# Third batch: crossbar transposes on SyncE's queue in place of TensorE transposes

## The chip, the cores and the metric

One core of one Trainium2 chip runs the whole program. The metric is device time in microseconds, the median of a few runs. A profiled execution has a span of its own, from the first to the last instruction, and a time of its own, which is a little longer. Engines are named as the profile names them: PE (TensorE matmuls), PEld (weight loads), DVE (VectorE), ACT (ScalarE), POOL (GpSimd), SP (SyncE). A name with a q (SPq, ACTq) is the engine's sequencer, which issues DMAs.

## The reference

A retention layer without softmax, then a two-layer network with a swish of learned slope. There are 8 batches, 8 heads, 576 positions and 64 columns for each head. Flattened, that is 4608 tokens of 512 columns.

```python
scores = scale * np.matmul(q, k.transpose(0, 1, 3, 2))
gamma = 1.0 - 2.0 ** (-5.0 - np.arange(H, dtype=np.float32))
Dmat = np.where(rel >= 0, gamma[:, None, None] ** rel[None, :, :], 0.0)
attn = np.matmul(scores * Dmat, v)
x = attn.transpose(0, 2, 1, 3).reshape(B * S, H * D)
h = x @ w_in                            # 512 -> 2048
out = (h * sigmoid(beta * h)) @ w_out   # 2048 -> 512
```

## The kernel before

The decay `gamma ** (s - t)` is split into a factor for the query and one for the value, so that only the causal mask is left between them. Each batch has 512 main positions, in four chunks of 128, and a tail of 64; two tails make a chunk of their own. The list `seq` numbers all chunks: batch b, chunk c is number 4b + c up to number 15, then come two tail chunks, and so on. The third batch, batch 2, has the chunks 8 to 11, taken as two pairs, (8, 9) and (10, 11). Chunks within a batch are joined by a state of 64x64 for each head, which `a_st` sums up and ScalarE copies into one of three buffers `sbds`.

For one batch the work is this. `load_q` (L81) fetches the queries in two DMAs of 512 KB, `load_kv` (L94) fetches keys and values of one chunk in two DMAs of 256 KB, all on SyncE's queue. POOL scales the queries (`pre_q`, L247), casts the keys (`pre`, L273) and scales the values (L255). Then queries and keys are turned, so that the head's columns lie on partitions. There are two ways to do that:

- On TensorE: `t_q` (L297) makes 8 transposes and one copy from PSUM (L298), twice in a batch, once with the copy on ScalarE and once with it on VectorE. `t_k` (L303) makes 4 transposes for one chunk and one copy on ScalarE (L304).
- By a DMA through the crossbar: `x_q` turns half the queries of a batch, `x_k` a pair of key chunks, `x_tail` a chunk of tails. All call `turn` (L281), which issues one transpose of 256 KB from ScalarE's queue.

The constant `XB = 3` says from which batch on the second way is taken. Then `first` does `a_st` and the scores `a_sc` of a pair (L323, masked by VectorE at L333), and `outputs` does for all four chunks `a_O` (L366), `a_cross` (L351, needs the states in `sbds`) and `a_x` (L384), the copy of the result to `xT`, on ScalarE for chunk 1 of a batch and on VectorE for the others.

The network's two layers are the bulk: `up` (L413) with its swish on ScalarE (L415), `down` (L426) with its copy on VectorE (L433) and its store on SyncE's queue (L436). Together they are the list `fill`. The order of all instructions on all engines is fixed by hand: `merged` walks through `fill`, and ahead of the entry of index n it emits every step of the other streams whose place is at most n. Each engine, and each DMA queue, takes its instructions in that order, and an instruction that waits holds back those behind it on the same engine. The indices that matter here: `d0` = 16 is the first `down` of batch 0, whose last entries for its four blocks of rows are at 25, 26, 27 and 31; `u1` = 32 is the first `up` of batch 1, in halves of 256 columns up to index 51; 58 to 73 are the `down` of batch 1, with stores after 61, 65, 69 and 73; `base[2]` = 74 is the first `up` of batch 2.

In the kernel before, the third batch has these places. POOL emits `pre_q(2)` at 41 to 44 and `pre` of chunks 8 to 11 at 46.5 to 48. `t_q` is at 47.5 and 48.5, `t_k` at 49.5, 50.5, 58.5 and 59.5, `first(8)` at 53, `a_st(9)` at 55, `first(10)` at 62, `outputs(8)` at 67. For the fourth batch, `load_q(3)` is at 47, `load_kv(12)` and `load_kv(13)` at 49 and 51, `pre_q(3)` at 57 to 60, `pre(12)` and `pre(13)` at 61 and 62, `x_q(3, 0)` at 63, `x_q(3, 1)` at 64.5, `x_k(3, 0)` at 66.5, `first(12)` at 77.

Of the kernel before, what the change touches and what calls it, by code (L numbers as in the profile page):

```python
# [19 lines left out]
def kernel(  # L20
# [10 lines left out]
    nc = tc.nc  # L31
# [9 lines left out]
    CB = MB // P  # L41
# [25 lines left out]

    NQ = 6
    E = CB
    XB = 3  # L70
    QB = 2
    q_tiles, kv_tiles = {}, {}

# [158 lines left out]
    batch, pair, live = {}, {}, {}  # L232
# [44 lines left out]
    def heads(t, p):  # L277
        return t[:, 2 * p:2 * p + 2, :].rearrange("p h d -> p (h d)")

    def turn(dst, src):  # L280
        nc.scalar.dma_start_transpose(dst.rearrange("p j pr s -> p (j pr) s"), src.rearrange("p j h d -> p (j h d)"))  # L281

    def x_q(b, u):
        turn(batch[b]["qT"][:, 2 * u:2 * u + 2], batch[b]["qs"][:, 2 * u:2 * u + 2])

    def x_k(b, u):
        kn, kT = pair[b, u]
        turn(kT, kn)

    def x_tail(i):  # L290
        turn(live[i]["qkT"], live[i]["qk"])
# [122 lines left out]
                             start=(ko == 0), stop=(ko == KO - 1))  # L414
        nc.scalar.activation(gts[m][:, fo, :, w], ph, ACT.Silu, scale=beta_sb[:, fo:fo + 1])  # L415

    pos_, ots = {}, {}

    def down(m, ms, f0, fn=4, n0=0, nn=d_model):

        gT = gts[m]
        if f0 == 0:
            pos_[ms] = psum.tile([P, d_model], F32, name="po", tag="mm", bufs=3)
        po = pos_[ms]
        for fo in range(f0, f0 + fn):
            nc.tensor.matmul(po[:, :nn], gT[:, fo, ms, :], w_out_sb[:, fo, n0:n0 + nn],  # L426
                             start=(fo == 0), stop=(fo == FO - 1))
        if f0 + fn < FO:
            return
        if ms == 0:  # L430
            ots[m] = stage.tile([P, MB // P, d_model], F32, name="ot", tag="wt", bufs=4)
        ot = ots[m][:, ms, n0:n0 + nn]
        nc.vector.tensor_copy(ot, po[:, :nn])  # L433
        if m < B:
            rows = out[m * S:m * S + MB].rearrange("(s i) n -> s i n", i=CB)
            nc.sync.dma_start(rows[:, ms, n0:n0 + nn], ot)  # L436
        else:
            for x in range(2):
                r0 = (2 * ms + x) * S + MB
                nc.sync.dma_start(out[r0:r0 + TL, n0:n0 + nn], ot[x * TL:(x + 1) * TL])  # L440
# [12 lines left out]
    def F(f, *a):  # L453
        return lambda: f(*a)
# [49 lines left out]
    fill = [F(up, 0, fo) for fo in range(FO)]  # L504
    d0 = len(fill)
    fill += [F(down, 0, ms, f0) for f0 in range(0, FO, 4) for ms in range(3)]
    fill += [F(down, 0, 3, f0) for f0 in range(0, FO, 4)]

    u1 = len(fill)
    fill += [F(up, 1, fo, 2 * x, 2) for x in range(2) for fo in range(10)]  # L510
    fill += [F(up, 1, fo) for fo in range(10, FO)]
    fill += [F(down, 1, ms, f0) for ms in range(MB // P) for f0 in range(0, FO, 4)]
    base = {1: u1 + 10}
    for n, m in enumerate(blocks[2:], 2):
# [6 lines left out]
    def second(i):  # L521
        for f in (a_O, lambda j: a_cross(j, False), a_x):
# [6 lines left out]
               [(d0 - 4 + 3.3 * g, F(cast_w_out, g)) for g in range(WG)],  # L529
               [(10.3, F(load_q, 1))] + [(10.3, F(load_kv, CB + n, (j,))) for n, j in keys_first],  # L530
               [(10.4, F(load_q, 2))] + [(10.4, F(load_kv, 2 * CB + n)) for n in range(2)],
               [(d0 + 8.6, F(load_kv, 2 * CB + 2)), (d0 + 10.1, F(load_kv, 2 * CB + 3))],
               [(d0 + 7, F(pre_q, 1, n)) for n in range(4)] + [(d0 + 10.6, F(t_q, 1, 0)), (d0 + 12.6, F(t_q, 1, 1))],
               [(d0 + 8, F(pre, 4, (0,))), (d0 + 8, F(pre, 5, (0,))), (d0 + 9, F(pre, 4, (1,))), (d0 + 9, F(pre, 5, (1,))),
                (d0 + 12.7, F(t_k, 4)), (d0 + 12.8, F(t_k, 5)), (d0 + 13.8, F(a_sc, 4)), (d0 + 13.81, F(a_sc, 5)),
                (d0 + 14.8, F(a_st, 4)), (d0 + 15.9, F(second, 4))],
# [16 lines left out]
    def pair_prep(i, at):  # L553
        b, c = seq[i]
        if b is None:
            return [(at - 31, F(load_tail, c)), (at - 21.5, F(pre, i)), (at - 21, F(load_tail, c + 1)),
                    (at - 13, F(pre, i + 1)), (at - 12, F(x_tail, i)), (at - 9.5, F(x_tail, i + 1))]
        n, st = full.index(i), []
        if b < XB:
            if c == 0:  # L560
                st += [(at - 12 + x, F(pre_q, b, x)) for x in range(4)]
                st += [(at - 5.5, F(t_q, b, 0)), (at - 4.5, F(t_q, b, 1))]
                st += [(at - 6.5 + x / 2, F(pre, i + x)) for x in range(CB)]
            return st + [(at - 3.5, F(t_k, i)), (at - 2.5, F(t_k, i + 1))]
        if c == 0:
            st += [(at - 30, F(load_q, b))] + [(at - 20 + x, F(pre_q, b, x)) for x in range(4)]
            st += [(at - 14 + 1.5 * x, F(x_q, b, x)) for x in range(2)]
        return st + [(at - 28, F(load_kv, n)), (at - 26, F(load_kv, n + 1)), (at - 16, F(pre, i)),
                     (at - 15, F(pre, i + 1)), (at - 10.5, F(x_k, b, c // 2))]

    todo = list(range(2 * CB, len(seq), 2))
    for n in range(1, B - 1):

        take = [i for i in todo if seq[i][0] == n + 1 or n == B - 2 or seq[i] == (None, 0) and n == CB - 1]
        todo = todo[len(take):]
        lo, hi = (base[n] + 11, base[n + 1] - 12) if n == 1 else (base[n] + 3, base[n + 1] - 8)
        at = [lo + x * (hi - lo) / (len(take) - 1) for x in range(len(take))]
        if len(take) == 2 and n > 1:
            at[1] -= 6
        for i, t in zip(take, at):  # L580
            st = pair_prep(i, t) + [(t, F(first, i))]
            if seq[i][0] is None:
                st.append((t + 5, F(second, i)))
            elif seq[i][1] == 0:
                st.append((t + 2, F(a_st, i + 1)))
            else:
                st.append((t + 5, F(outputs, i - 2)))
            streams.append(st)
# [32 lines left out]
```

## Time and profile before

| What | Value |
|---|---|
| median of 3 runs | 311.66 us (311.6 to 312.2) |
| the profiled execution: its time | 311.92 us |
| the profiled execution: its span | 310.1 us |
| granted TensorE clock, mean | 0.998 |
| ACT busy | 143.0 us (46%) |
| DVE busy | 106.9 us (34%) |
| POOL busy | 96.0 us (31%) |
| transposes of queries on PE, L297 | 48, of them 16 in batch 2 |
| transposes of keys on PE, L303 | 48, of them 16 in batch 2 |
| crossbar transposes on ACT's queue, L281 | 24 |

PE's own rows count a matmul from its start to its modelled end, and matmuls overlap; so the time that a group takes from PE is read from the chain of waits, where pieces follow one another without overlap. In a row of the timeline the columns are start, duration, engine, line, operation, output<-input, and the number of instructions merged; in brackets is the idle time ahead of it and what ended that. For a DMA the duration is that of its issue on the sequencer; the time to landing is told apart.

### The profile page before, as it was taken

The numbers are of one execution on the slowest core, as the hardware profiler recorded it, in microseconds if no ns is written. First come the engines' busy times: TensorE is split into PE (matmuls) and PEld (weight loads), VectorE is DVE, ScalarE is ACT, GpSimd is POOL, SyncE is SP. The second block draws the span as 40 slices with busy tenths as digits, with TensorE's granted clock in tenths as the row PEclk, the third lists the DMA queues.
The fourth block names the chain that finished last, engine by engine and source line by source line (L and its number), as shares of the span: only waits on it lengthen the run. The fifth ranks groups of instructions, "written<-read, shape, count | busy, mean of one in ns | idle before, by whom it ended". The sixth has DMA issues, their size and how long they took to land.

```text
span 310.1 us, 5363 instructions
## 1 busy us (share of the span) xinstructions
PE 298.5 (96%) x2144; PEld 157.8 (51%) x2177; DVE 106.9 (34%) x191; ACT 143.0 (46%) x256; POOL 96.0 (31%) x131
## 2 busy tenths in 40 slices
PE   7789999999999999999999999999999999999995
PEld 5544456775544454454554545455545444444444
DVE  7554476342531342434430434043405420010012
ACT  5567626995138412560186117711673037207700
POOL 4663026846524282254308031902420000000000
PEclk9999999999999999999999999999999999999999
DMA  8999999998989999999897697968852110031011
GB/s 207 221 355 387 380 232 273 233 257 179 202 197 162 224 189 235 218 212 198 133 234 107 136 205 207 201 115 192 196 76 37 68 70 0 17 88 34 0 70 68
DMA packets 123897, 52.79 MB, mean 170 GB/s; under 512 B 105680, under 2 KB 116320, under 8 KB 123872
## 3 DMA queue, kind: packets, MB, share of 16 engines
q1 hardware_dynamic: 98496, 46.15, 61.5%
q10 hardware_dynamic: 25376, 6.30, 13.6%
q8 instruction: 17, 0.28, 0.4%
q14 instruction: 8, 0.07, 0.1%
HBM read 36.71 MB, written 9.44 MB: 149 GB/s over the span
## 4 chain that ended last, share of the span: by engine, by line
PE 85%; DMA 6%; SPq 5%; DVE 1%; issue 1%; ACT 1%; POOL 1%; POOLq 0%
PE po L426 40%; PE ph L413 35%; DMA wt<-in_moe_w_in_dram 4%; SPq L94 3%; PE O L366 3%; PE sc L323 3%; DMA qn<-in_q_dram 2%; PE O L351 2%; PE st L396 2%; SPq L178 1%; POOL qs L247 1%; PE T L297 1%; PE T L303 1%; ACT gT L415 0%; DVE xT L384 0%
## 5 line engine op out<-in xcount | busy, mean ns | idle before, releaser
L415 ACT ACTIVATE gT<-ph,beta_sb 128x512 bf16<-128x512 f32 (+1 forms) x154 | 99.2, 659 | 86.3 <-PE ph L413 83.4
L413 PE MATMUL ph<-xT,w_in_sb 128*128 128x512 bf16 (+1 forms) x600 | 129.3, 365 | 3.2 <-DVE w_in_sb L186 0.9
L426 PE MATMUL po<-w_out_sb,gT 128*128 128x512 bf16 (+2 forms) x591 | 126.7, 368 | 1.1 <-issue 0.3
L413 PEld LDWEIGHTS <-w_in_sb 128*128 128x128 bf16 x616 | 58.7, 98 | 65.0 <-DVE w_in_sb L186 2.3
L426 PEld LDWEIGHTS <-gT 128*128 128x128 bf16 x608 | 57.1, 98 | 62.5
L333 DVE TENSOR_TENSOR R<-sc,causal 128x512 bf16<-128x512 f32 x71 | 44.3, 684 | 68.9 <-PE sc L323 68.9
L433 DVE COPY ot<-po 128x512 f32<-128x512 f32 (+2 forms) x38 | 25.0, 662 | 92.1 <-PE po L426 92.0
L255 POOL TENSOR_TENSOR vn<-kvn,gv 128x512 bf16<-128x512 f32 x32 | 33.4, 1042 | 22.8 <-DMA kvn<-in_v_dram 11.5
L247 POOL TENSOR_TENSOR qs<-qn,gq 128x512 bf16<-128x512 f32 x24 | 24.3, 1042 | 33.2 <-DMA qn<-in_q_dram 33.2
L273 POOL CAST kn<-kvn 128x512 bf16<-128x512 f32 x32 | 19.6, 612 | 47.7 <-DMA kvn<-in_k_dram 47.3
L401 ACT CAST sbd<-st 64x256 bf16<-64x256 f32 x48 | 17.4, 362 | 15.0 <-PE st L396 14.3
L384 DVE CAST xT<-O 128x512 bf16<-128x512 f32 x24 | 15.8, 688 | 19.6 <-PE O L366 9.6
L384 ACT CAST xT<-O 128x512 bf16<-128x512 f32 x11 | 6.4, 586 | 32.2 <-PE O L351 25.2
L396 PE MATMUL st<-vn,kn 128*128 128x128 bf16 x128 | 12.4, 219 | 0.2 <-POOL vn L255 0.2
L396 PEld LDWEIGHTS <-kn 128*128 128x128 bf16 x128 | 9.3, 98 | 5.0 <-issue 0.2
L366 PE MATMUL O<-R,vn 128*64 128x128 bf16 x288 | 10.7, 221 | 0.0
L323 PE MATMUL sc<-qT,kT 64*128 64x128 bf16 x256 | 10.3, 217 | 0.4 <-ACT kT L304 0.2
L366 PEld LDWEIGHTS <-vn 128*64 128x64 bf16 x288 | 8.5, 110 | 4.1 <-issue 3.6
L323 PEld LDWEIGHTS <-kT 64*128 64x128 bf16 x288 | 8.1, 94 | 3.8 <-ACT kT L304 1.5
L304 ACT COPY kT<-T 128x512 bf16<-128x512 bf16 x12 | 6.9, 586 | 4.8 <-PE T L303 4.8
L208 PE MATMUL ph<-warm 128*128 128x128 f32 (+1 forms) x24 | 7.0, 429 | 1.2 <-DVE warm L119 1.2
L186 DVE CAST w_in_sb<-wt 128x256 bf16<-128x256 f32 (+1 forms) x14 | 6.0, 476 | 5.2 <-DMA wt<-in_moe_w_in_dram 5.2
(56 smaller groups left out, 90.2 us busy)
## 6 DMA issues: line engine op xcount, KB each, us to landing
qn<-in_q_dram SPq DMA_DIRECT2D x16, 512.0 KB, 5.8
kvn<-in_k_dram SPq DMA_DIRECT2D x32, 256.0 KB, 5.9
kvn<-in_v_dram SPq DMA_DIRECT2D x32, 256.0 KB, 5.6
out_dram<-ot SPq DMA_DIRECT2D x31, 256.0 KB, 2.7
wt<-in_moe_w_out_dram SPq DMA_DIRECT2D x4, 1024.0 KB, 9.5
wt<-in_moe_w_in_dram SPq DMA_DIRECT2D x4, 512.0 KB, 7.5
wt<-in_moe_w_in_dram SPq DMA_DIRECT2D x2, 1024.0 KB, 11.8
out_dram<-ot SPq DMA_DIRECT2D x9, 128.0 KB, 2.4
```

The source lines that it names most:

```text
L247: e.tensor_tensor(batch[b]["qs"][:, cs, hs], q_tiles[b][:, hs, cs].rearrange("p h i d -> p i h d"), gq[:, cs, hs].unsqueeze(3).to_broadcas ...
L255: nc.gpsimd.tensor_tensor(live[i]["vn"][:], kv_tiles.pop(i)[:, 1], gains(gv, c), ALU.mult)
L273: nc.gpsimd.tensor_copy(kn[:, c % 2], t[:, 0])
L323: nc.tensor.matmul(view(sc[j][:, p, :]), L["kT"][r, p, :], rhs, start=True, stop=True, skip_group_check=True)
L333: nc.vector.tensor_tensor(R[:, j], sc[j][:], causal4[:] if i == CB - 1 else m_b, ALU.mult)
L366: nc.tensor.matmul(O[j * D:(j + 1) * D, p, :], vn[:, 2 * p + j, :], R[:, j, p, :], start=p == 0 and not (early and crossed), stop=early or ...
L384: (nc.scalar.copy if on_act else nc.vector.tensor_copy)(x, O[:])
L396: nc.tensor.matmul(st[:, p, :], heads(L["kn"], p), heads(L["vn"], p), start=(c == 0 and p == 0), stop=True, skip_group_check=True)
L413: nc.tensor.matmul(ph, w_in_sb[:, ko, fo * P:(fo + 1) * P], xts[m][:, ko, :, w], start=(ko == 0), stop=(ko == KO - 1))
L415: nc.scalar.activation(gts[m][:, fo, :, w], ph, ACT.Silu, scale=beta_sb[:, fo:fo + 1])
L426: nc.tensor.matmul(po[:, :nn], gT[:, fo, ms, :], w_out_sb[:, fo, n0:n0 + nn], start=(fo == 0), stop=(fo == FO - 1))
L433: nc.vector.tensor_copy(ot, po[:, :nn])
```

## The change

`XB` becomes 2, so the third batch takes the crossbar way, but its four transposes are issued from SyncE's queue, while those of the later batches stay on ScalarE's. They have places of their own: the two of the queries at 28.6 and 28.7, that of the first pair of keys at 29.6, that of the second pair at 41. POOL's `pre_q(2)` goes to 28.5, `pre` of chunks 8 and 9 to 29 and 30, of 10 and 11 to 40 and 40.5. The four stores of batch 0's `down` are no longer issued where they arise, but kept in a list `held`; `release` issues what is in it, at 29.7 and at 33. `load_kv(11)` goes from 26.1 to 29.8. `t_q` and `t_k` of the third batch are gone. `first(8)` goes from 53 to 58, `a_st(9)` from 55 to 60, `first(10)` from 62 to 64, `outputs(8)` from 67 to 69.

```diff
-    XB = 3
+    XB = 2
...
-    def turn(dst, src):
-        nc.scalar.dma_start_transpose(dst.rearrange("p j pr s -> p (j pr) s"), src.rearrange("p j h d -> p (j h d)"))
+    def turn(dst, src, on_sp=False):
+        (nc.sync if on_sp else nc.scalar).dma_start_transpose(dst.rearrange("p j pr s -> p (j pr) s"), src.rearrange("p j h d -> p (j h d)"))
...
-        turn(batch[b]["qT"][:, 2 * u:2 * u + 2], batch[b]["qs"][:, 2 * u:2 * u + 2])
+        turn(batch[b]["qT"][:, 2 * u:2 * u + 2], batch[b]["qs"][:, 2 * u:2 * u + 2], b == XB)
...
-        turn(kT, kn)
+        turn(kT, kn, b == XB)
...
+    pos_, ots, held = {}, {}, []
+
+    def release():
+        while held:
+            nc.sync.dma_start(*held.pop(0))
...
-            nc.sync.dma_start(rows[:, ms, n0:n0 + nn], ot)
+            if m == 0:
+                held.append((rows[:, ms, n0:n0 + nn], ot))
+            else:
+                nc.sync.dma_start(rows[:, ms, n0:n0 + nn], ot)
...
-               [(d0 + 8.6, F(load_kv, 2 * CB + 2)), (d0 + 10.1, F(load_kv, 2 * CB + 3))],
-               [(d0 + 7, F(pre_q, 1, n)) for n in range(4)] + [(d0 + 10.6, F(t_q, 1, 0)), (d0 + 12.6, F(t_q, 1, 1))],
+               [(d0 + 8.6, F(load_kv, 2 * CB + 2)), (d0 + 12.6, F(x_q, XB, 0)), (d0 + 12.7, F(x_q, XB, 1)),
+                (d0 + 13.6, F(x_k, XB, 0)), (d0 + 13.7, F(release)), (d0 + 13.8, F(load_kv, 2 * CB + 3)),
+                (u1 + 1, F(release))],
+               [(d0 + 7, F(pre_q, 1, n)) for n in range(4)] + [(d0 + 12.5, F(pre_q, XB, n)) for n in range(4)] + [(d0 + 10.6, F(t_q, 1, 0)), (d0 + 12.6, F(t_q, 1, 1))],
...
-        if b < XB:
+        if b == XB:
             if c == 0:
-                st += [(at - 12 + x, F(pre_q, b, x)) for x in range(4)]
-                st += [(at - 5.5, F(t_q, b, 0)), (at - 4.5, F(t_q, b, 1))]
-                st += [(at - 6.5 + x / 2, F(pre, i + x)) for x in range(CB)]
-            return st + [(at - 3.5, F(t_k, i)), (at - 2.5, F(t_k, i + 1))]
+                return [(d0 + 13, F(pre, i + x, (0,))) for x in range(2)] + \
+                       [(d0 + 14, F(pre, i + x, (1,))) for x in range(2)]
+            return [(u1 + 8 + x / 2, F(pre, i + x)) for x in range(2)] + [(u1 + 9, F(x_k, b, 1))]
...
-        lo, hi = (base[n] + 11, base[n + 1] - 12) if n == 1 else (base[n] + 3, base[n + 1] - 8)
+        lo, hi = (base[n] + 16, base[n + 1] - 10) if n == 1 else (base[n] + 3, base[n + 1] - 8)
```

More of the change, by code (lines that the diff above doesn't have):

```diff
@@ L415, in up @@
         nc.scalar.activation(gts[m][:, fo, :, w], ph, ACT.Silu, scale=beta_sb[:, fo:fo + 1])
-    pos_, ots = {}, {}
+    pos_, ots, held = {}, {}, []
+    def release():
+        while held:
+            nc.sync.dma_start(*held.pop(0))
     def down(m, ms, f0, fn=4, n0=0, nn=d_model):
```

## The prediction

> **What bounds the kernel now.** I read the engines' shares first, then the busy time by stretch, then the chain of waits around the third batch.
>
> ```profile
> PE 298.5 (96%) x2144; PEld 157.8 (51%) x2177; DVE 106.9 (34%) x191; ACT 143.0 (46%) x256; POOL 96.0 (31%) x131
> 58.00:70.00 12.00, 11.82 (x124) 8.85 (x122) 3.87 (x6) 10.80 (x25) 7.53 (x10) 1.00 1.02 258
> 70.00:76.00 6.00, 5.95 (x45) 3.15 (x46) 0.26 (x1) 3.48 (x7) 3.16 (x4) 1.00 0.97 210
> 76.00:93.00 17.00, 16.84 (x143) 8.89 (x141) 7.84 (x13) 4.54 (x10) 7.30 (x9) 1.00 0.98 184
> ```
>
> In the stretches the columns after the length are PE, PEld, DVE, ACT, POOL, then the clock, the DMA share and GB/s. From 58 to 93 us PE is idle for 0.39 of 35 us, at full clock: the order of work is such that PE never waits. So what leaves PE is won, and any wait put into PE's stream is lost. The DMA engines are as full as PE (shares 0.97 to 1.02): what is added there makes later transfers later. The chain shows what the third batch's transposes take from PE:
>
> ```profile
> 62.24 0.45 PE T L297 x8
> ...
> 63.12 0.45 PE T L297 x8
> ...
> 64.00 0.22 PE T L303 x4
> ...
> 64.76 0.22 PE T L303 x4
> ...
> 72.40 0.39 PE T L303 x4
> ...
> 73.65 0.22 PE T L303 x4
> ```
>
> **What is removed.** 32 transposes: 0.45 + 0.45 + 0.22 + 0.22 + 0.39 + 0.22 = 1.95 us (by 32 x 0.056, 1.8; the rest is a pause at 72.4). With them go copies: ACT 1.01 + 4 x 0.58 = 3.3 us, DVE 0.69 us. I cost these at nothing, since PE waits for neither here; ACT's 10.80 of 12 us in 58 to 70 only gets looser.
>
> **What is added.** Four DMA issues on SP, and 4 x 256 KB through full DMA engines. On ACT's queue such an issue took 1.25 to 3.5 us and landed after 3.0 to 10.1 us:
>
> ```profile
> L281 ACTq DMA_TRANSPOSE kT<-kn x14: 1247/1288/3514, 80.0 to 233.1; - x14
> DMA to landing us min/median/max: 3.0/5.0/10.1
> q10 hardware_dynamic: 25376, 6.30, 13.6%
> ```
>
> No row has one on SP's queue. Each one's share of the full engines lies between 1.1 us (issue and landing of `load_kv` in the full queue follow at 1.1 us, same bytes) and 2.0 us (of the 11.8 us of transfers from 78.0 to the last landing at 89.8, which moved three transposes, two stores and four key or value loads, 1.1 us a load and 0.7 a store, whose landings follow at 0.5 and 0.8 us, leave 6.0). Over the whole run it is 13.6% of 310.1 / 24 = 1.76. I take 1.6, nearer to the mean than to the short end because three come in a row. The Trainium skill (Advanced Engine Details and Errata, X-Bar Transpose) holds that transposing DMAs are as fast as ordinary ones; the 1.76 against 1.1 says otherwise for this mix, and by the page the four would cost 4.4 instead of 6.4 us.
>
> **What is moved: SP's queue.** This is how it ran:
>
> ```profile
> 56.49 1.11 SPq L94 DMA_DIRECT2D kvn<-in_k_dram  x1
> 57.65 1.07 SPq L94 DMA_DIRECT2D kvn<-in_v_dram  x1
> 58.81 1.46 SPq L436 DMA_DIRECT2D out_dram<-ot  x2
> 60.36 0.42 SPq L94 DMA_DIRECT2D kvn<-in_k_dram  x1
> ...
> 61.83 2.72 SPq L436 DMA_DIRECT2D out_dram<-ot  x2
> 64.60 2.04 SPq L81 DMA_DIRECT2D qn<-in_q_dram  x2
> ```
>
> Up to 58.7 nothing changes; POOL's order hardly changes either, since `pre_q(2)` (55.17 to 59.21) already followed chunk 7. Now come, behind the values of chunk 10, which land 4.6 us after their issue, at 62.3: two query transposes (their input is there at 57.2 and 59.2, so SP hardly waits), the first key transpose (chunk 9 cast by 60.4), three stores, the keys of chunk 11. Landings: 62.3 + 3 x 1.6 = 67.1, + 3 stores x 0.7 = 69.2, + 1.1 = 70.3 for keys 11, against 65.4 before. The cast takes 0.6, so the second key transpose, which needs it, is issued about 71.1. **This is the new wait**: until then SP stands, and behind it stand `load_q(3)`, the loads of chunks 12 and 13 and the next store. `load_q(3)` goes from 64.60 to about 72.4. The queue has then drained, so the second half of the queries lands 5.3 us after its issue (as the pair issued at 102.6 and 103.0 in a drained queue) or a little more, at 78.5, where it was 72.7. With 1.1 and 2.0 us a transpose these come 1.5 us earlier and 1.2 to 2 us later. The held stores cost nothing: SP's next store waits for DVE, and it waited 9.6 us for DVE's `ot` between 55 and 95. If that cover were gone they would shift `load_kv(11)` by their 2.1 us, which is counted.
>
> **What is due when.** PE's new places follow from the chain: `first(10)` at 75.60 + 2 entries x 0.865 - 1.78 = 75.55, `outputs(8)` at 80.65, its last `a_cross` at 82.2, `up` of batch 2 at 88.86 - 1.95 = 86.9, the scores of chunk 12 at 91.67 - 1.95 = 89.7. Before, these were the ends of what was wanted:
>
> ```profile
> 72.84 4.04 POOL L247 TENSOR_TENSOR qs<-qn,gq 128x512 bf16<-128x512 f32 x4 [4.37 <-DMA qn<-in_q_dram]
> 76.04 2.50 ACTq L281 DMA_TRANSPOSE qT<-qs  x1
> 80.01 3.51 ACTq L281 DMA_TRANSPOSE kT<-kn  x1
> 83.57 0.58 ACT L384 CAST xT<-O 128x512 bf16<-128x512 f32 x1 [6.89 <-POOL kn L273]
> ```
>
> 1. Keys 10 and 11 for `first(10)`: issued 71.1, + 3.5 us (three transposes at 112.8 to 116.1 landed after 3.4 to 3.6) = 74.6, due 75.8. Met by 1.2; late by 0.8 at the slow end.
> 2. ACT's order turns round: `x_q(3, 0)` at 63 now stands ahead of `first(10)`'s state copies at 64. It needs half of `pre_q(3)`: 78.5 + 0.1 + 2.04 = 80.6, + 1.28 of issue, + 2 x 0.37 of copies = 82.7, due 82.2: **0.5 us late** (1.7 with an issue of 2.5).
> 3. `x_k(3, 0)` follows after all of `pre_q(3)` and the casts of chunks 12 and 13: 78.6 + 4.04 + 0.6 + 1.04 + 0.6 = 84.9, against 80.0. Behind it ACT has chunk 9's `xT` copy: 84.9 + 1.3 + 0.6 = 86.8, due 86.9: just met.
> 4. The keys of chunk 12: it took 9.7 us from issue at 80.0 to landing at 89.7, two before `first(12)`. With 3.5 us 84.9 becomes 88.4, with 9.7 it becomes 94.6; due 89.7. Of the batch's three, it now follows the first by 4.3 us (before 4.0), and behind it the five issued from 97.0 to 121.5 landed after 3.4 to 5.6; between these ends, and nearer to the latter, I take 6: 90.9, **1.2 us late**.
>
> The delays don't add: a wait at 2 moves the later dates too, so the largest counts. After that there is room again: the next transposes at 96.97 and 112.8 stood at their places in ACT's order, not at their inputs. Sum: -1.95 + 1.2 = -0.75 us. The profiled execution's time, 311.92, becomes 311.2; it stands 0.26 above the median, so on the median the forecast is **310.9 us**.
>
> The Trainium skill (DMA: Bandwidth & Descriptors, Silent corruption) has a rule that speaks against the change: of two transposing streams, the later one's first transpose must wait until the earlier stream has landed fully. No trace here has two such streams. By it `x_q(3, 0)` on ACT would wait for the second key transpose, landing at 74.6 by step 1; it is held until 80.6 anyway, so the sum stays the same unless that landing slips by 6 us.
>
> **Rivals.**
> - **No wait at all** (20%): 311.66 - 1.95 = 309.7. For it: with 1.1 us a transpose every date moves 1.5 us earlier and only step 4 with a slow landing could be late. Against it: the mean of 1.76.
> - **The fourth batch's keys come late** (36%), the slower side: `load_q(3)` waits on SP behind a cast that waits for keys 11, and PE waits ahead of `first(12)`. With step 4's 9.7 us the wait is 94.6 - 89.7 = 4.9, the time 311.66 - 1.95 + 4.9 = 314.6; with a landing of 8 us it is 3.2 and 312.9. It decides the sign from a landing of 84.9 + x > 89.7 + 1.95, x = 6.8 us, on. For it: DMA share 0.98 in 76 to 93, and 9.7 in the row of before. Against: 3.4 to 5.6 us for the five issued from 97.0 to 121.5. I take 313.6 for it.
> - **The transposes on PE were free** (10%): PE in 62 to 66 was paced by ACT's half-width swish (0.48 us each against 0.44 of PE), so their loss gains nothing: 311.7. Against: the copies leave ACT at the same stroke, and no wait for ACT stands in the chain there.
>
> **How the numbers follow.** A measurement of this kernel tells a difference from none at about 0.2%, 0.6 us. The forecast has 34%, with its own range 310.3 to 311.5; I give 24 of it to faster and 10 to same. With the rivals that is faster 24 + 20 = 44%, same 10 + 10 = 20%, slower 36%. The range goes from 309.6 (no wait) to 314.2, which takes most of the third case in.
>
> **What would show it.** L297 and L303 at 32 instead of 48 each; four rows of transposes on SPq, the last issued near 71, and `load_q(3)` right behind it near 72; `qs` of batch 3 near 78.6 instead of 72.84; PE idle ahead of a late `a_cross` near 82, for ACT's `sbd`, and ahead of `first(12)` near 90, for a DMA. If keys 11 land after 73, or a transpose on SP's queue takes 2.5 us of it, the third case holds; if `load_q(3)` goes out before 70, the second.

## The result, and the profile after

| | before | after |
|---|---|---|
| median of 20 runs | 311.88 us (311.21 to 312.85) | 313.97 us (311.42 to 316.1) |
| ratio, 95% interval | | 1.0062 [1.0045, 1.0079] |
| profiled execution: time, span | 311.92, 310.1 us | 313.69, 311.9 us |
| transposes L297 and L303 on PE | 96 | 64 |

The changed kernel is slower by 0.6%, and its runs are spread wider. The ratio leaves out its run of 316.1 us, which counts as a slow one. Six of its 20 runs have a mean granted clock of 0.994 or 0.995 and took 314.2 to 316.1 us; the median of the 14 others is 313.4. Experiment 3 shows what such a clock comes with.

The busy time by stretch, in the columns of before (length, then PE, PEld, DVE, ACT, POOL, clock, DMA share, GB/s), of the changed kernel:

```profile
58.00:70.00 12.00, 11.88 (x107) 8.00 (x102) 0.90 (x2) 10.27 (x22) 5.56 (x7) 1.00 1.18 208
70.00:76.00 6.00, 6.00 (x46) 3.07 (x48) 2.97 (x5) 1.28 (x4) 1.65 (x2) 1.00 0.79 163
76.00:93.00 17.00, 14.17 (x114) 7.14 (x108) 6.54 (x10) 4.46 (x10) 8.82 (x10) 1.00 1.23 243
```

Up to 76 PE is as full as before, with less to do: it is ahead by what the transposes took. From 76 to 93 it stands for 2.8 of 17 us, where before it stood for 0.16. Its timeline in the changed kernel says for what (idle time ahead and what ended it, in brackets):

```profile
83.93 0.40 PE L351 MATMUL O<-qT,sbd 128*128 128x128 bf16 x4 [1.67 <-ACT sbd L401]
...
89.06 2.75 PE L413 MATMUL ph<-xT,w_in_sb 128*128 128x512 bf16 x12 [0.20 <-ACT xT L384]
...
94.18 0.62 PE L323 MATMUL sc<-qT,kT 64*128 64x128 bf16 x16 [2.15 <-DMA kT<-kn]
```

First the last `a_cross` of the third batch waits for a state copy, then the scores of chunk 12 wait for the fourth batch's keys: 1.67 + 0.20 + 2.15 = 4.0 us. These scores come at 94.18; before, they came at 91.61 in the same view. Of the difference of 2.57 us, -1.78 (32 transposes) + 4.02 = 2.24 is accounted for, and 0.3 is in smaller pieces. By the end 0.8 comes back (the spans differ by 1.8 only); 0.6 of it is visible: before, PE waited 0.6 us near 165 for ACT, whose issue of a transpose at 162.17 took 2.29 us; the same issue took 1.25 after.

SP's queue and the chain of waits of the changed kernel show the inputs' way (start and duration; behind a DMA its time from issue to landing):

```profile
58.83 3.40 SPq L281 DMA_TRANSPOSE qT<-qs  x2
62.33 1.27 SPq L281 DMA_TRANSPOSE kT<-kn  x1
63.70 2.13 SPq L421 DMA_DIRECT2D out_dram<-ot  x3
65.87 0.44 SPq L94 DMA_DIRECT2D kvn<-in_k_dram  x1
66.36 0.85 SPq L94 DMA_DIRECT2D kvn<-in_v_dram  x1
67.32 2.37 SPq L421 DMA_DIRECT2D out_dram<-ot  x1
71.76 1.25 SPq L281 DMA_TRANSPOSE kT<-kn  x1
73.06 1.17 SPq L81 DMA_DIRECT2D qn<-in_q_dram  x2
```

```profile
65.87 5.20 DMA kvn<-in_k_dram
...
73.69 5.76 DMA qn<-in_q_dram
...
85.80 8.33 DMA kT<-kn
```

`load_q(3)` goes out at 73.06 (before 64.60) and lands at 79.45 (before 72.7). The transpose of chunk 12's keys goes out at 85.80 (before 80.01) and lands at 94.13 (before 89.70). ACT's timeline of the changed kernel has the turned order between:

```profile
81.69 1.33 ACTq L281 DMA_TRANSPOSE qT<-qs  x1
83.11 0.76 ACT L401 CAST sbd<-st 64x256 bf16<-64x256 f32 x2 [10.22 <-DVE xT L384]
...
85.80 2.58 ACTq L281 DMA_TRANSPOSE kT<-kn  x1
88.42 0.59 ACT L384 CAST xT<-O 128x512 bf16<-128x512 f32 x1 [4.55 <-issue]
```

The state copies, which have their input from PE at about 76, run at 83.11, when `x_q(3, 0)` ahead of them has got its queries from POOL and been issued.

### The profile page after: what moved, and what is told of

It is laid out like the page before. It is cut to its first block, busy times and chain, and to the rows that moved or that the text cites. A ratio compares the mean times of both kernels' runs of the same rounds, so it can differ in the third digit from the quotient of the medians.

```text
span 311.9 us, 5335 instructions
## 1 busy us (share of the span) xinstructions
PE 299.8 (96%) x2145; PEld 156.8 (50%) x2145; DVE 105.8 (34%) x190; ACT 140.6 (45%) x251; POOL 96.7 (31%) x131
## 4 chain that ended last, share of the span: by engine, by line
PE 78%; DMA 10%; SPq 6%; POOL 3%; issue 1%; DVE 1%; ACT 0%; POOLq 0%
PE po L430 36%; PE ph L413 34%; DMA wt<-in_moe_w_in_dram 4%; SPq L94 3%; DMA kT<-kn 3%; PE sc L323 3%; PE O L366 2%; DMA qn<-in_q_dram 2%; DMA kvn<-in_k_dram 2%; PE O L351 2%; PE st L396 1%; POOL qs L247 1%; POOL vn L255 1%; SPq L178 1%; POOL kn L273 1%
## 5 line engine op out<-in xcount | busy, mean ns | idle before, releaser
L430 PE MATMUL po<-w_out_sb,gT 128*128 128x512 bf16 (+2 forms) x608 | 128.9, 368 | 0.0
L351 PE MATMUL O<-qT,sbd 128*128 128x128 bf16 x96 | 7.4, 220 | 2.0 <-ACT sbd L401 1.7
```

## The experiments

Two theories were to be told apart. Theory 1: SP stands still for the cast of chunk 11, and `load_q(3)` stands behind it. Theory 2: it is the traffic, four more transposes through full DMA engines. All experiments were timed beside runs of the kernel before, whose medians were 311.73 to 311.81. Each has one profile. In a line on PE's waits the three numbers are the total in us, how many there were, and the longest.

**1. Queries first.** Edit to the changed kernel:

```diff
-            return [(u1 + 8 + x / 2, F(pre, i + x)) for x in range(2)] + [(u1 + 9, F(x_k, b, 1))]
+            return [(u1 + 8 + x / 2, F(pre, i + x)) for x in range(2)] + [(u1 + 16, F(x_k, b, 1))]
```

> The transpose of the second pair of keys goes behind load_q(3) on SP's queue (place 48 instead of 41). Theory 1, SP stands still for that transpose's input and load_q(3) stands behind it: load_q(3) goes out near 69.7 instead of 73.06 and lands near 75.5 instead of 79.45, PE's waits of 1.7 (state copies) and 2.1 us (keys of chunk 12) go, at most 1 us comes up ahead of first(10), since these keys now land near 76.5; 310 to 311 us. Theory 2, the four transposes' share of full DMA engines is what delays the fourth batch, whoever stands: load_q(3) lands at 78 or later all the same and the time stays at 313 to 314.

Measured: 312.75 us, ratio 1.0027 [1.0005, 1.0049]. `load_q(3)` goes out at 70.27 and lands at 77.09, between the two expectations. PE's one wait from 60 to 100 in this kernel:

```profile
PE sc L323 <- DMA kT<-kn: 2.8, 1, 2.8
```

It stands in `first(10)`, ahead of the scores: the second pair of keys, now behind the queries, lands at 78.18, not at 76.5. The keys of chunk 12 land at 92.47 and are used at 92.52. So half of the loss goes, and a wait for one transfer is traded for a wait for another. Neither theory is right alone.

**2. Second pair of keys on TensorE.**

```diff
-            return [(u1 + 8 + x / 2, F(pre, i + x)) for x in range(2)] + [(u1 + 9, F(x_k, b, 1))]
+            return [(u1 + 8 + x / 2, F(pre, i + x)) for x in range(2)] + [(u1 + 28.5, F(t_k, i)), (u1 + 29.5, F(t_k, i + 1))]
```

> The second pair of keys of the third batch goes back to TensorE (8 transposes, two ScalarE copies); the other three crossbar transposes stay. Theory 1: SP has nothing to stand for, load_q(3) goes out near 69.7, the waits go; the gain is 1.95 less 0.45 on PE, so 310.2 to 311. Theory 2: three quarters of the traffic stays, so of the 3.8 us of waits some 2.8 stay: 312.8 to 313.5.

Measured: 312.29 us, 1.0018 [0.9992, 1.0044]; the interval holds no change. `load_q(3)` goes out at 70.75, with nothing to stand for; the keys of chunk 12 land at 92.70, and PE still waits 1.8 us for them. Nearer to theory 2: without any stand the loss shrinks, but the gain doesn't come.

**3. State copies first.**

```diff
-            st += [(at - 14 + 1.5 * x, F(x_q, b, x)) for x in range(2)]
+            st += [(at - (12.8 if b == 3 else 14) + (0.3 if b == 3 else 1.5) * x, F(x_q, b, x)) for x in range(2)]
```

> x_q(3, 0) goes behind first(10) in ScalarE's order (64.2 instead of 63), so the state copies no longer wait for it. The wait of 1.7 us ahead of the last a_cross goes. If the waits don't add, because both hang on the same late load_q(3), the wait for the keys of chunk 12 grows by as much, from 2.1 to 3.8, and the time stays at 313.5 to 314.3. If they add, the time is 312.0 to 312.5.

Measured: 313.8 us, 1.0069 [1.0044, 1.0095]: the time stays. The wait for the state copies is gone, but in its profile PE now stands before `up` of batch 2, for the `xT` copy that is behind `x_k(3, 0)` on ACT:

```profile
PE ph L413 <- ACT xT L384: 2.4, 1, 2.4
```

The keys of chunk 12 land at 93.56 here, and PE takes them at 93.60 without a wait. That is because PE was slow on the way there: behind the wait it has a lower clock. The first line is from its timeline, the second is the busy time by stretch, with the clock third from the end:

```profile
88.93 4.44 PE L413 MATMUL ph<-xT,w_in_sb 128*128 128x512 bf16 x12 [2.44 <-ACT xT L384]
89.00:93.00 4.00, 4.00 (x12) 1.45 (x12) 0.00 (x0) 1.88 (x4) 1.04 (x1) 0.58 1.28 261
```

The same 12 matmuls took 2.75 us in the changed kernel, at full clock; with that PE would have come for the keys near 91.9 and waited 1.7 us. So this profile has 2.4 us of wait and 1.7 us of lower clock where the changed kernel's has 4.0 us of waits. The waits don't add; each stands for the same late load, and ACT's order only chooses where it is seen. The place that was expected was not the right one.

**4. Four more transposes.** Edit to the kernel before:

```diff
+    spare = {}
+
+    def idle_turn(x):
+        if x == 0:
+            spare[0] = stage.tile([P, 4, 2 * HP, P], BF16, name="spare", tag="wt", bufs=4)
+        src = w_in_sb[:, x, :1024]
+        nc.sync.dma_start_transpose(spare[0][:, x], src)
+
+    streams.append([(d0 + 12.6, F(idle_turn, 0)), (d0 + 12.7, F(idle_turn, 1)), (d0 + 13.6, F(idle_turn, 2)),
+                    (u1 + 9, F(idle_turn, 3))])
```

> The kernel before, with four more transposes of 256 KB on SP's queue at the changed kernel's places, from data that has long been there into a spare tile that nobody reads: traffic and issue, no gain, nothing to stand for. Theory 2: load_q(3) lands 6 us later (four times 1.5), near 78.7, the keys of chunk 12 land near 94, PE waits 3 to 4 us, 315 to 316. Theory 1: the rest of the queue closes up, PE waits under 1.5 us, 312 to 313.3.

Measured: 311.38 us, 0.9969 [0.995, 0.9988]: no loss, even slightly faster. Yet the traffic does what theory 2 said: `load_q(3)` goes out at 71.82 and lands at 77.84, 5.2 us later than before. The keys of chunk 12 land at 89.67, after 5.5 us, and PE takes them at its old place, in this kernel's timeline:

```profile
92.00 0.62 PE L323 MATMUL sc<-qT,kT 64*128 64x128 bf16 x16
```

So the added transfers and the late queries alone cost nothing. The keys themselves are not late here (89.67, before 89.70), so this run doesn't tell what late keys cost a PE that isn't early, and why they landed after 5.5 us here and after 8.3 in the changed kernel stays open. Where the 0.3% of gain comes from was not settled; PE's wait near 165 is 0.3 us here.

**5. Fourth batch later, and 6, its control.** The first edit went into both kernels, the changed one and the one before; the other two into the changed one alone.

```diff
-            st = pair_prep(i, t) + [(t, F(first, i))]
+            st = pair_prep(i, t)
+            t += 5 * (i == 3 * CB)
+            st += [(t, F(first, i))]
...
-            st += [(at - 14 + 1.5 * x, F(x_q, b, x)) for x in range(2)]
+            st += [(at - (12.8 if b == 3 else 14) + (0.3 if b == 3 else 1.5) * x, F(x_q, b, x)) for x in range(2)]
...
-                     (at - 15, F(pre, i + 1)), (at - 10.5, F(x_k, b, c // 2))]
+                     (at - 15, F(pre, i + 1)), (at - (7.5 if i == 3 * CB else 10.5), F(x_k, b, c // 2))]
```

> The changed kernel, with the use of the fourth batch's first pair later: first(12) at 82 instead of 77, a_st(13) at 84; on ScalarE x_q(3, 0) behind first(10) (64.2) and x_k(3, 0) behind outputs(8) (69.5). Nothing is taken off SP's queue or the DMA engines. If the loss is only that PE, 1.95 us earlier, meets inputs that come 4 to 5 us later, the waits of 1.7 and 2.1 us go: keys of chunk 12 land near 94, due near 89.7 + 5 x 0.865 = 94.0. 309.5 to 310.5. If the stretch is bound by the DMA engines as such, the wait only moves to a later place: 312.5 or more.

> The kernel before with the same later places of first(12) and a_st(13), nothing else: a control. Its keys of chunk 12 landed 2 us before their use, so nothing is won: 311.4 to 312.1. If it is faster by over 0.6 us, the later place is worth something of its own and e5's gain isn't the change's.

Measured: 309.99 us (309.58 to 310.34), 0.9934 [0.9921, 0.9948], and for the control 312.33 us, 1.0014 [0.9994, 1.0034]. The keys of chunk 12 land at 93.94, as late as in the changed kernel; PE comes for them at 94.26. The inputs' lateness is untouched, the wait is gone, and so is the loss. The control gains nothing, so the later place is worth nothing of its own. The two edits of ACT's order are not in the control; the first of them alone, in the changed kernel, is experiment 3 and gained nothing there; the second was not run alone. What is left in the profile of experiment 5 from 60 to 100 is

```profile
PE st L396 <- ACT sbd L401: 0.7, 1, 0.7
```

at 97.40, behind the issue of `x_k(3, 1)` on ACT at 95.15; the control has the same wait with 0.6.

**7. Nothing to stand for.** Edit to the changed kernel, in `x_k`:

```diff
+        if (b, u) == (XB, 1):
+            nc.sync.dma_start_transpose(kT.rearrange("p j pr s -> p (j pr) s"), w_in_sb[:, 0, :1024])
+            return
         turn(kT, kn, b == XB)
```

> The changed kernel, with the transpose of the second pair of keys reading data that has long been there, so SP never stands for the cast of chunk 11; the same traffic at the same place. Chunks 10 and 11 get scores from other numbers. Theory 1 (the stand costs it): load_q(3) goes out near 70.5 instead of 73.06, keys of chunk 12 land 2.5 us earlier, near 91.6, time 311.5 to 312.3. Theory 2 (traffic): load_q(3) lands within 1 us of 79.45 all the same and the time is 313 to 314.3. Between: the parts' shares.

Measured: 314.33 us, 1.0076 [1.0049, 1.0102]. The time doesn't come back, against theory 1. SP's queue in this kernel:

```profile
68.50 2.44 SPq L424 DMA_DIRECT2D out_dram<-ot  x1
71.04 1.30 SPq L289 DMA_TRANSPOSE kT<-w_in_sb  x1
72.39 1.16 SPq L81 DMA_DIRECT2D qn<-in_q_dram  x2
```

The transpose follows the store at once, at 71.04; in the changed kernel it goes out at 71.76, and `load_q(3)` is 0.7 us earlier here. That is not the price of the stand: in this profile the queue was late already, for the store goes out at 68.50, against 67.32 in the changed kernel, where it is issued by 69.69 and SP then stands for 2.1 us. `load_q(3)` lands at 78.31, 1.1 us earlier than in the changed kernel, so time and landing are both just outside what theory 2 allowed. The transpose of chunk 12's keys goes out 1.05 us earlier (84.75), but takes 9.1 us to land instead of 8.3, so the keys come at 93.84, only 0.3 earlier. The stand is real; what its removal won at the queries was lost again at the landing of the keys.

**8. Without holding back.**

```diff
-            if m == 0:
+            if m < 0:
                 held.append((rows[:, ms, n0:n0 + nn], ot))
```

> The changed kernel without holding back: batch 0's four stores are issued where they arise, so three of them stand ahead of the query transposes. These go out some 2 to 3 us later and the first pair of keys lands near 69.5, just when first(8) wants it near 69.7: a wait of 0 to 1 us there; keys 11 and all behind them come at about the same time as in the changed kernel, since the same transfers lie ahead of them. 313.5 to 315.

Measured: 313.84 us, 1.0058 [1.0039, 1.0077]: as the changed kernel. The first pair of keys lands at 68.69 and PE doesn't wait for it. Holding the stores back is worth nothing that this shows.

**9. PE freed alone.** Edit to the kernel before; `t_q` likewise, with `qT`:

```diff
     def t_k(i):
+        if seq[i][0] == 2:
+            nc.vector.memset(live[i]["kT"], 0.01)
+            return
```

> The kernel before, with the third batch's 32 transposes on TensorE and their copies left out: VectorE fills the turned queries and keys of that batch with a constant in their place (its scores come from that). PE is freed as by the change, no transfer is added and all places are those of before. If the change's gain is worth what the chain showed, and only the later inputs eat it: 1.95 us less, and since the keys of chunk 12 landed at 89.70 and are then due at 89.7, a wait of 0 to 0.6: 309.7 to 310.4. If freeing PE there gains nothing: 311.4 to 312.

Measured: 309.95 us, 0.9955 [0.9937, 0.9973]. The transposes on PE are worth 1.8 of the 1.95 us that the chain showed, when no transfer is added. The keys of chunk 12 land at 85.16, earlier than before, and PE doesn't wait.

**10. The fourth batch at 81.** Edit to the kernel of experiment 5:

```diff
-            t += 5 * (i == 3 * CB)
+            t += 4 * (i == 3 * CB)
...
-                st.append((t + 2, F(a_st, i + 1)))
+                st.append((t + (0.4 if i == 3 * CB else 2), F(a_st, i + 1)))
```

> As the kernel with the fourth batch's first pair later (first(12) at 82, a_st(13) at 84), but at 81 and 81.4, so that the state copies of both stand ahead of x_k(3, 1) in ScalarE's order, whose wait of 1.25 us of issue held the first of them in that kernel and PE for 0.7 us. Keys of chunk 12 land near 93.9, due near 93.2: a wait of 0.7 may take the place of it, or the two states follow too close: 309.3 to 310.1. If both come, 310.5.

Measured: 309.7 us (309.46 to 310.53), 0.9941 [0.9922, 0.9959]. The wait for the state copy is gone, and 0.5 us for the keys has come. The two can't be told apart by time; both beat the kernel before and the changed one. The stretch that lost 2.8 us in the changed kernel is full, at a higher DMA share than either had:

```profile
76.00:93.00 17.00, 17.00 (x127) 8.56 (x122) 6.44 (x10) 5.54 (x11) 8.97 (x11) 1.00 1.28 244
```

## Why the prediction was wrong

The forecast was 310.9 us, faster; measured is 313.97, slower. The time lies in the range, and the second rival (the fourth batch's keys come late, 313.6 us, 36%) is what happened, so the error is in which of the two was held likelier. The signs that were named for this rival did not show (keys 11 after 73, or 2.5 us for a transpose; measured 71.07 and 1.5): the loss came from a landing that these signs do not look at.

- **What leaves PE.** 1.95 us by the chain; experiment 9 gives 311.73 - 309.95 = 1.8. Right, and with it the third rival (free on PE) falls.
- **Landings up to keys 11.** Forecast 67.1 for the three transposes and 70.3 for the keys; measured 66.75 and 71.07. A transpose took (66.75 - 62.27) / 3 = 1.5 us of the full engines, forecast 1.6. Right.
- **SP's stand.** Forecast issue at 71.1, then `load_q(3)` at 72.4 and landed at 78.5; measured 71.76, 73.06 and 79.45. The times were right, within 1 us, the weight of the reason not: SP did stand, from 69.69 to 71.76, but with nothing to stand for `load_q(3)` still lands 5.2 us late in experiment 4 and 5.6 in experiment 7, of the 6.8. Most of its lateness is the traffic ahead of it.
- **Step 1**, keys 10 and 11: landing 74.85 (forecast 74.6), in time. Right, with some luck: the issue was 0.7 us later and the landing 0.4 us shorter than forecast.
- **Step 2**, the state copies behind `x_q(3, 0)`: forecast 0.5 us late, measured 1.67. The issue came at 81.69 instead of 80.6 and took 1.33; the direction was right. The size is that of the slow end (1.7), but for another reason: late queries, not an issue of 2.5 us.
- **Step 3**, the `xT` copy behind `x_k(3, 0)`: forecast just met, measured 0.20 late. Right.
- **Step 4 is the step that failed.** The prediction took 6 us from issue to landing for the keys of chunk 12, "between these ends, and nearer to the latter", against 9.7 in the row of before. It took 8.33, over the 6.8 from which by the prediction's own count the sign turns, and the issue came 0.9 later: 94.13 instead of 90.9, for a due time of 89.7. The keys were 4.4 us late instead of 1.2. Of these 3.2 us 0.8 come back by the end, which leaves about the 2.5 us by which the profiled execution misses its forecast (313.69 against 311.2). The five quick rows that the prediction leaned on end at 121.45; the next transpose of the same trace, issued at 123.18, took 10.1 us. Over the kernels this one transfer took 9.7 us before, 8.1 to 9.1 in experiments 1, 2, 3, 6, 7 and 8, 5.5 in experiment 4, 5.9 in 9, and 6.3 to 6.5 where it was issued later (5 and 10). What sets the length of the landing isn't shown.
- **The clock** is not in the sum. Without the six runs of lower clock the changed kernel's median is 313.4 instead of 313.97, so some 0.5 us of the miss of 3.1 us on the medians go with it.
- **"The delays don't add"** held: the waits sum to 4.0 us, the lateness of the keys against the due time is 4.4, and experiment 3 moved the waits to another place without a change in time.
- **The two transposing streams.** By the rule of the Trainium skill's page (DMA: Bandwidth & Descriptors, Silent corruption) ACT's `x_q(3, 0)` may start only when SP's last transpose has landed. It landed at 74.85, and `x_q(3, 0)` went out at 81.69, when its queries were there; the rule cost nothing here.

What the change did, in one line: it put 1.8 us less on PE ahead of a point whose inputs had 2 us to spare, and at the same time made those inputs 4.4 us later. Freeing PE alone gains 1.8 us (experiment 9, where the keys came at 85.16), the transfers alone cost nothing (experiment 4, where the keys came no later than before), together they cost 2.1 us, and the loss goes when that point is moved by four or five entries (5 and 10).

## What to carry to other kernels

Taking work off the bounding engine moves every later due time forward, so list what had slack behind that point; a gain of 1.8 us uses up the 2 us that an input had to spare, and from then on any delay of that input is a wait, unless its use is moved as well. When transfers are added to a full queue, shift the use of what comes behind them by as much as they delay it (five entries, 4.3 us, here). For a landing in a crowded stretch take the spread of the rows of that transfer at that place (5.5 to 9.7 us here) and plan for its slow end, not for the rows of a quieter stretch.

## What the runs showed of the hardware

- In the crowded stretch an earlier issue did not mean an earlier landing: issued between 84.58 and 87.45, the transpose of chunk 12's keys landed between 93.56 and 94.13 in six kernels (the changed one and experiments 3, 5, 7, 8 and 10). In experiments 1, 2 and 4 it went out at 83.43, 84.61 and 84.18 and landed at 92.47, 92.70 and 89.67.
- A crossbar transpose landed 3.1 us after issue in a drained queue (71.76 to 74.85) and 5.5 to 9.7 us, mostly over 8, when stores and loads of the other queue ran beside it (the keys of chunk 12 in all kernels); three in a row on SP's own full queue cost 1.5 us each on average.
- After a long wait of PE its clock can be low for some us. In the profiles of experiments 3 and 8 PE goes on at 88.93 and 93.68 after waits of 2.4 and 2.5 us, and the granted clock is 0.58 in 89 to 93 and 0.51 in 94 to 97.5. The profiles of the changed kernel and of experiments 1 and 7, with waits of 2.2, 2.8 and 2.4 us, have 1.00 behind them, so it doesn't always come. Of the 72 runs of the kernels with a wait of 1.8 us or more (the changed one, 1, 2, 3, 7 and 8), 30 have a mean clock of 0.993 to 0.995; of the 35 runs of experiments 4, 5, 6 and 10, with no wait over 0.7 us from 27 us on, none has. Long waits are not the only case: 3 of the 11 runs of experiment 9 have such a mean, in whose profile the clock is 0.51 in 9 to 12.5, and so have 8 of 72 runs of the kernel before.
